# Moving one product of the second matmul stage into the first, with a new order of the rest, in a fused attention and MLP kernel

## The chip, the core and the metric

The kernel runs on one core of a Trainium2 chip. The core has five engines, each with its own queue of instructions in program order: TensorE (PE, with weight loads as PEld), VectorE (DVE), ScalarE (ACT), GpSimd (POOL) and SyncE (SP), which here issues the transfers. They meet only at semaphores. Matmuls write to PSUM, eight banks of 128 x 512 float32, from which VectorE and ScalarE read. The metric is the device time of one execution in microseconds (us).

## What is computed

Attention inside chunks of 64 tokens, then an MLP with exact Gelu over all tokens:

```python
q_c = q.reshape(B, H, nc, chunk, D)          # B, H, S, D = 8, 8, 576, 64; chunk = 64
scores = scale * np.matmul(q_c, k_c.transpose(0, 1, 2, 4, 3))
attn = np.exp(scores - np.max(scores, axis=-1, keepdims=True))
attn = attn / (np.sum(attn, axis=-1, keepdims=True) + 1e-09)
out = np.matmul(attn, v_c)
...
h = x @ w_in                                 # x: 4608 x 512, w_in: 512 x 2048
g = 0.5 * h * (1.0 + erf(h * inv_sqrt2))
return (g @ w_out).astype(np.float32)        # w_out: 2048 x 512
```

x is the attention output with its eight heads side by side.

## The kernel before

**Tiles.** The 4608 tokens are nine tiles of 512 (t = 0 to 8, so the fourth to eighth are t = 3 to 7). Tile t < 8 holds eight of the nine chunks of batch t; the ninth tile gathers the last chunk of all batches. While the MLP of tile t runs, the attention of tile t + 1 is fitted in between, so that its x is ready for the next tile, and with `quad_S` the scores of tile t + 2.

**Two stages.** `mm1_groups` computes h with Gelu, then `mm2_seven` (from t = 3) the output rows. Both use a block scheme in which a 2 by 2 block product takes seven products instead of eight, with sums of blocks formed beforehand (of x: `x_sums`; of w_in and w_out: once; of h: `h_sums` in three parts h1 to h3, `h_third`, `h_fourth`) and sums of results afterwards. In mm1 the columns of h fall into four groups a to d, each with seven products of four matmuls (128 x 256). In mm2 each of the seven products is 16 matmuls of that size.

**mm1's order** is written out as a string of words (`FOUR` for t = 3 to 8, line 639), which line 686 walks. `3b` is product 3 of group b on TensorE; products 1, 2 go to the group's bank X, 3, 5, 6 to Y, 4, 7 to Z. `c1b` is ScalarE's copy of X to Y, `c2b` and `c3b` are copies of Y to SBUF (ScalarE, VectorE), `a1b` and `a2b` are VectorE's adds of Z to those, `g12b` is a Gelu on ScalarE that writes a quarter of the group's h (g11 from X, g12 from Y, g21 and g22 from the sums that a2 and a1 leave). `h1` to `h3` (lines 576, 577) are VectorE's sums of h that mm2's second and third factors need. The order of the words is the order of each engine's queue.

**mm2's order** (line 761 on). The banks X, Y, Z, W are taken in turn from the pool `ps_mm`, which has three banks and which mm1 uses for its four Y banks (a, b, c, d) before. So X reuses the bank of group b's Y, read last by g12b, Y that of c, Z that of d, and W that of X. Before the change, with the lines:

- X1 (781): the first product, into X; then ScalarE copies X to Y (782), so that both can go on from the same term.
- hook 1: `act_table(Exp)`, then `rows_av` (line 334: 64 small matmuls on TensorE, attention times v of the next tile, into two `ps_tp` banks, three `ps_at` banks and mm2's Z bank) and `rows_x` (line 352: for each of these six banks a reciprocal and a multiply on VectorE; after the third and the sixth bank a transpose by DMA on SP writes half of x).
- `h_third` on VectorE; Y2 (787) into Y, and ScalarE copies it to s2 (788).
- X2 (789) into X, ScalarE copies it to y (790), SP stores it.
- Y1 (792) into Y, ScalarE copies it to s5 (793); `h_fourth`.
- hook 2: loads of later tiles on SP. Z (796) into Z; between its two halves, from t = 4 on, hook (2, 0): `quad_S`, 64 small matmuls for the scores of tile t + 2 into two `ps_tp` and two `ps_at` banks, their exponentials on ScalarE, `act_table(Gelu)`. At t = 3 it stands ahead of Z. VectorE adds Z to s2 (797).
- W (800) into a new bank; VectorE adds it to s5 and s2 (801, 802), SP stores. hook 4: `x_sums` of the next tile.
- Y4 (805) into Y; ScalarE copies it to y, SP stores.

The last tile goes through `last_seven` instead. The eighth (t = 7) has no `quad_S`, as no tile t + 2 is left.

**Pools that set waits.** `ps_mm` three banks, `ps_at` three, `ps_tp` two. The tiles `y_sb` (two), `x_t` (one, shared by the rows that `rows_x` writes and the sums of x), h (one), and one buffer for each sum of h.

Of the kernel before, what the change touches and what calls it, by code (L numbers as in the profile page):

```python
# [11 lines left out]
def kernel(  # L12
# [10 lines left out]
    P = 128  # L23
    f32 = mybir.dt.float32
# [327 lines left out]
    def rows_x(t):  # L352

        st = tiles[t]
        rows = work.tile([P, 2, 2 * G, 2, D], bf16, tag="x_t", name="x_r", bufs=1)
        xT = by_halves(t).rearrange("p s g (n e) -> p s (g n) e", e=P)
        for bank in range(6):
            s, b0 = bank // 3, NX * (bank % 3)
            nb = min(NX, 2 * G - b0)
            av = st["av"][bank][:, :2 * nb]  # L360
            one = work.tile([P, 2 * NX], f32, tag="one", name="one", bufs=2)
            nc.vector.reciprocal(one[:, :2 * nb], av[:, :, D])
            nc.vector.tensor_tensor(rows[:, s, b0:b0 + nb].rearrange("p b r d -> p (b r) d"), av[:, :, :D],
                                    one[:, :2 * nb].to_broadcast([P, 2 * nb, D]), op=mybir.AluOpType.mult)
            if bank % 3 == 2:
                nc.sync.dma_start_transpose(xT[:, s], rows[:, s].rearrange("p b r d -> p (b r d)"))
# [248 lines left out]
    def x_sums(t, which=(1, 3, 2, 4)):  # L615
# [7 lines left out]
        for i in which:  # L623
# [17 lines left out]
               g22c 4d g12c g12b 3d a2c a2d g21c g22d g12d g21d h2 h3"""  # L641

    FOURS = range(FIRST7, NT)
    PROGRAMS = {1: LATE, 2: THIRD, **{t: FOUR for t in FOURS}}

    def mm1_groups(t, extra, between={}):
# [39 lines left out]
        for word in PROGRAMS.get(t, PROGRAM).split():  # L686
# [71 lines left out]
    def halves(bank):  # L758
        return [bank[:, 0], bank[:, 1]]

    def mm2_seven(t, at={}):

        def also(i):
            for u in at.get(i, ()):
                u()
        st = tiles[t]
        h = st["h"][:].rearrange("p (k f) (m e) -> p k f m e", k=2, m=2)
        w = w_out_sb[:].rearrange("p (k f) (n e) -> p k f n e", k=2, n=2)
        T = [None] + [w_t[i] for i in range(1, 5)]
        def bank_mm():  # L770
            return ps_mm.tile([P, 2, NH], f32, tag="mm", name="y_ps")
# [10 lines left out]
        AC(Y[:], X[:])  # L782
# [12 lines left out]
        also(2)  # L795
        product(halves(Z), h[:, 1, :, 1], T[4], True, lambda m: also((2, m)))
        TT(s2[:], Z[:], s2[:], op=add)
        also(3)
# [166 lines left out]
    with tc.manual_schedule():  # L965
# [126 lines left out]
        for t in range(1, NT):  # L1092
# [30 lines left out]
            elif n < NT:  # L1123
# [91 lines left out]
```

## Time and profile before

| | us |
|---|---|
| median of three executions | 271.12 |
| lowest, highest | 270.23, 272.2 |
| the profiled execution | 270.41 |
| its span, first to last instruction | 268.6 |
| TensorE busy | 259.6 (97%) |
| VectorE busy | 202.1 (75%) |
| ScalarE busy | 187.1 (70%) |
| GpSimd busy | 77.0 (29%) |

The profile is one execution. A row of its timeline has the start from the span's beginning, the duration, the engine, the kernel's line, the operation, output and input by the program's names with the shape, and how many instructions were merged; in brackets how long the engine stood before it and what ended that. A bar of matmuls shows also the pipeline's tail, so successive bars overlap; the step from one start to the next is the slot that TensorE spends. The chain of waits follows the work that ended last back from the end, at each step to what released it. The granted clock of TensorE is given in tenths for 40 slices of the span.

In the middle of the span the tiles repeat each 26.3 us (Y2 starts at 149.67 in one and at 175.94 in the next).

### The profile page before, as it was taken

How to read it: one execution, taken by the hardware profiler on the slowest of the kernel's cores; microseconds unless marked ns; L12 is line 12 of the kernel's file. 1: busy time of each engine (PE TensorE's matmuls, PEld its weight loads, DVE VectorE, ACT ScalarE, POOL GpSimd, SP SyncE). 2: the span in 40 equal slices, each digit the busy share in tenths (PEclk: the TensorE clock that was granted, in tenths of full speed). 3: DMA queues.
4: the chain of work that ended last, by engine and by line, in shares of the span. 5: the costliest groups of instructions: out<-in, count | busy, mean ns of one | idle time of the engine just before them, and what ended most of it. 6: DMA issues, size and time to landing. Idle time of an engine off the chain costs nothing.

```text
span 268.6 us, 7554 instructions
## 1 busy us (share of the span) xinstructions
PE 259.6 (97%) x3077; PEld 195.6 (73%) x3092; DVE 202.1 (75%) x372; ACT 187.1 (70%) x364; POOL 77.0 (29%) x130
## 2 busy tenths in 40 slices
PE   7989999999999999999999999999999999999993
PEld 3554454476548654888888888888888888888882
DVE  2565775989997879589569956995699769958961
ACT  3466756797767967897689669957995799239700
POOL 3735667361440061441044103500362030000000
PEclk9999999999999999999999999999999999999998
DMA  7999999997979959999899989988886760430005
GB/s 230 285 377 402 395 388 243 237 286 194 336 205 261 244 123 231 279 237 191 232 232 231 177 216 242 264 152 206 237 193 146 166 192 0 89 138 12 2 2 156
DMA packets 127075, 56.59 MB, mean 211 GB/s; under 512 B 103488, under 2 KB 120896, under 8 KB 127040
## 3 DMA queue, kind: packets, MB, share of 16 engines
q1 hardware_dynamic: 126592, 55.59, 79.4%
q10 hardware_dynamic: 448, 0.52, 0.7%
q8 instruction: 24, 0.39, 0.6%
q14 instruction: 11, 0.09, 0.1%
HBM read 36.70 MB, written 9.44 MB: 172 GB/s over the span
## 4 chain that ended last, share of the span: by engine, by line
PE 92%; ACT 2%; DVE 1%; DMA 1%; issue 1%; POOL 0%; SPq 0%; ACTq 0%; DVEq 0%; POOLq 0%
PE y_ps L746 24%; PE h_Y L677 15%; PE y_ps L866 12%; PE h_Z L677 10%; PE h_X L677 10%; PE h_ps L538 6%; PE y_ps L891 4%; PE y_ps L755 4%; PE s_ps L247 2%; PE h_ps L699 1%; DMA arrival<-in_k_dram 1%; PE tp L170 1%; ACT y_ps L782 1%; PE warm L958 1%; PE rc_ps L484 1%
## 5 line engine op out<-in xcount | busy, mean ns | idle before, releaser
L677 PEld LDWEIGHTS <-w_in_s 128*128 128x128 bf16 x480 | 46.8, 98 | 6.1
L677 PEld LDWEIGHTS <-w_in_sb 128*128 128x128 bf16 x360 | 35.1, 98 | 6.5
L677 PE MATMUL h_X<-x,w_in_sb 128*128 128x256 bf16 x240 | 33.7, 272 | 0.0
L677 PE MATMUL h_Y<-x_t,w_in_s 128*128 128x256 bf16 x240 | 32.7, 272 | 0.0
L866 PE MATMUL y_ps<-w_out_sb,h 128*128 128x512 bf16 x137 | 31.7, 379 | 0.9 <-issue 0.8
L746 PEld LDWEIGHTS <-h_s 128*128 128x128 bf16 x304 | 29.7, 98 | 3.6 <-issue 0.2
L746 PEld LDWEIGHTS <-h 128*128 128x128 bf16 x288 | 27.8, 98 | 3.4
L218 POOL CAST v_nat<-arrival 128x1024 bf16<-128x1024 f32 x14 | 14.8, 1061 | 48.4 <-DMA arrival<-in_v_dram 48.3
L164 POOL CAST q_nat<-arrival 128x512 bf16<-128x512 f32 x33 | 19.4, 627 | 28.2 <-DMA arrival<-in_q_dram 19.1
L164 POOL CAST k_nat<-arrival 128x512 bf16<-128x512 f32 x34 | 21.9, 678 | 14.0 <-DMA arrival<-in_k_dram 10.1
L746 PE MATMUL y_ps<-w_t,h_s 128*128 128x256 bf16 x208 | 24.8, 273 | 0.0
L866 PEld LDWEIGHTS <-h 128*128 128x128 bf16 x144 | 13.3, 98 | 15.0 <-issue 0.2
L746 PE MATMUL y_ps<-w_out_sb,h 128*128 128x256 bf16 x192 | 22.9, 273 | 0.0
L963 ACT ACT_TABLE_LOAD x16 | 20.5, 1283 | 1.0 <-PEq L1199 0.7
L684 ACT ACTIVATE h<-h_Y 128x512 bf16<-128x512 f32 x30 | 17.7, 595 | 2.4 <-PE h_Y L677 1.9
L714 ACT COPY h_Y<-h_X 128x512 f32<-128x512 f32 x30 | 17.0, 582 | 2.8 <-PE h_X L677 2.6
L684 ACT ACTIVATE h<-h_X 128x512 bf16<-128x512 f32 x30 | 17.8, 597 | 1.4 <-PE h_X L677 0.6
L677 PE MATMUL h_Z<-x_t,w_in_s 128*128 128x256 bf16 x120 | 18.0, 273 | 0.0
L677 PE MATMUL h_Y<-x,w_in_s 128*128 128x256 bf16 x120 | 17.7, 273 | 0.0
L677 PE MATMUL h_Z<-x_t,w_in_sb 128*128 128x256 bf16 x120 | 17.4, 272 | 0.0
L725 DVE COPY h_a<-h_Y 128x512 f32<-128x512 f32 x8 | 5.5, 692 | 14.1 <-PE h_Y L677 14.1
L254 ACT ACTIVATE pT<-s_ps 128x512 bf16<-128x512 f32 x28 | 14.5, 601 | 2.3 <-PE s_ps L247 2.3
(148 smaller groups left out, 489.4 us busy)
## 6 DMA issues: line engine op xcount, KB each, us to landing
arrival<-in_q_dram SPq DMA_DIRECT2D x7, 1024.0 KB
arrival<-in_k_dram SPq DMA_DIRECT2D x24, 256.0 KB
out_dram<-y_sb SPq DMA_DIRECT2D x23, 256.0 KB
arrival<-in_v_dram SPq DMA_DIRECT2D x20, 256.0 KB
arrival<-in_moe_w_out_dram SPq DMA_DIRECT2D x4, 1024.0 KB
arrival<-in_v_dram SPq DMA_DIRECT2D x30, 128.0 KB
out_dram<-y_sb SPq DMA_DIRECT2D x5, 512.0 KB
arrival<-in_moe_w_in_dram SPq DMA_DIRECT2D x4, 512.0 KB
```

Source lines behind the costliest of these rows:

```text
L164: copy(st[nm][:, g].rearrange("p j r d -> p r j d"), st[nm + "f"][:, 2 * g:2 * g + 2])
L218: copy(st["v"][:, part[0], part[1], :D], st["vf"][:, part[0], part[1]])
L254: nc.scalar.activation(pT[:].rearrange("p u (c j) -> p u c j", j=J), s_ps[g2][c][:].rearrange("p u (j c) -> p u c j", j=J), Act.Exp, scale ...
L538: nc.tensor.matmul(h_ps[a][:], w_in_sb[:, ks, f * P:(f + 1) * P], st["x"][:, ks, :], start=(ks == 0), stop=(ks == KS - 1))
L677: nc.tensor.matmul(banks[g + name][:, i], lhs[:, kk, i], rhs[:, kk], start=fresh and i == kk == 0, stop=(kk == 1), skip_group_check=True)
L684: nc.scalar.activation(h[:, j:j + 2, m], src[:], Act.Gelu)
L714: AC(banks[g + "Y"][:], banks[g + "X"][:])
L746: nc.tensor.matmul(out[m], lhs[:, f, m * P:(m + 1) * P], rhs[:, f, :], start=fresh and f == 0 and (m == 0 or len(out) == 3), stop=(f == FH ...
L755: nc.tensor.matmul(out[m], lhs[:, f, m * P:(m + 1) * P], rhs[:, f, :], start=False, stop=(f == FH - 1), skip_group_check=True)
L866: nc.tensor.matmul(y_ps[:], st["h"][:, f, ms * P:(ms + 1) * P], w_out_sb[:, f, :], start=(f == 0), stop=(f == FF - 1))
L891: nc.tensor.matmul(tiles[t]["y_ps", ms][:], tiles[t]["h"][:, f, ms * P:(ms + 1) * P], w_out_sb[:, f, :], start=(f == 0), stop=False)
L963: nc.scalar.activation(act_scratch[:], rest[:, 0:1], func)
```

## The change

For the tiles t = 3 to 7 a new program string `AHEAD` takes the place of `FOUR`. It is the same up to `c3d`. Behind that, products 3b, 3c, 4c come in this order, then the word `X`, which is mm2's first product (X1), then 4d and 3d. The word `cX` is ScalarE's copy of X to Y. The word h2 stands ahead of a2d, h3 at the end. `mm2_seven` then starts with X2, and its order becomes X2, AV, Y2, Z, Y1 (with `quad_S` between its halves, at t = 3 too), W, Y4. `h_third` follows Z's matmuls in program order, and `h_fourth` Z's add. The s5 copy of bank Y is on VectorE instead of ScalarE. In `rows_x` the bank order is 5, 3, 4, 0, 1, 2 (bank 5 is mm2's Z), in the tiles t + 1 = 4 to 8. The ninth tile keeps `FOUR` and `last_seven`.

```diff
-        for bank in range(6):
+        for at, bank in enumerate((5, 3, 4, 0, 1, 2)):
...
-            if bank % 3 == 2:
+            if at % 3 == 2:
                 nc.sync.dma_start_transpose(xT[:, s], rows[:, s].rearrange("p b r d -> p (b r d)"))
...
+    AHEAD = """begin 1a 1b c1a 1c 6a 7a c1b c2a 6b 5a 2a c1c 6c c2b 5b 7b c3a g11a a1a c3b c2c 3a a1b 1d 4a g22a 4b
+               g12a c1d 2b a2a g22b 6d 5c g21a a2b 2d 7c h1 g11b c3c c2d 2c g11d 5d a1c 7d c3d 3b g21b g11c 3c a1d
+               g22c 4c g12b X g12c a2c 4d g22d g21c cX h2 a2d 3d g12d g21d h3"""
...
-    PROGRAMS = {1: LATE, 2: THIRD, **{t: FOUR for t in FOURS}}
+    PROGRAMS = {1: LATE, 2: THIRD, **{t: AHEAD if t < B else FOUR for t in FOURS}}
...
+            elif word == "X":
+                mm2_first(t)
+            elif word == "cX":
+                st["Y"] = bank_mm()
+                AC(st["Y"][:], st["X"][:])
...
+    def mm2_first(t):
+        h, w = out_blocks(t)
+        tiles[t]["X"] = bank_mm()
+        product(halves(tiles[t]["X"]), h[:, 0, :, 0], w[:, 0, :, 0], True)
...
-        X, Y = bank_mm(), bank_mm()
+        X, Y = (st["X"], st["Y"]) if t < B else (bank_mm(), bank_mm())
...
-        also(0)
-        product(halves(X), h[:, 0, :, 0], w[:, 0, :, 0], True)
-        AC(Y[:], X[:])
         Z = bank_mm()
         st["Z"] = Z[:].rearrange("p m n -> p (m n)")
+        product_by_f(halves(X), h[:, 1, :, 0], w[:, 1, :, 0])
+        AC(y[0][:, :, :NH], X[:])
+        store(t, 0, 0, y)
         also(1)
-        h_third(t)
         product_by_f(halves(Y), h_sum(t, 2), T[2])
         AC(s2[:], Y[:])
-        product(halves(X), h[:, 1, :, 0], w[:, 1, :, 0], False)
-        AC(y[0][:, :, :NH], X[:])
-        store(t, 0, 0, y)
-        product(halves(Y), h_sum(t, 1), T[1], False)
-        AC(s5[:], Y[:])
+        product(halves(Z), h[:, 1, :, 1], T[4], True)
+        h_third(t)
+        TT(s2[:], Z[:], s2[:], op=add)
         h_fourth(t)
         also(2)
-        product(halves(Z), h[:, 1, :, 1], T[4], True, lambda m: also((2, m)))
-        TT(s2[:], Z[:], s2[:], op=add)
+        product(halves(Y), h_sum(t, 1), T[1], False, lambda m: also((2, m)))
+        DV(s5[:], Y[:])
         also(3)
...
-                    e2.setdefault(2 if t == FIRST7 else (2, 0), []).extend([lambda: quad_S(n + 1), lambda: act_table(Act.Gelu)])
+                    e2.setdefault((2, 0), []).extend([lambda: quad_S(n + 1), lambda: act_table(Act.Gelu)])
```

`TT` is VectorE's two-input operation, `DV` and `AC` are copies on VectorE and ScalarE, `product_by_f` walks the 16 matmuls by blocks of h's columns, both row halves in turn, and `product` one row half after the other.

More of the change, by code (lines that the diff above doesn't have):

```diff
@@ L759, in halves, with bank_mm, out_blocks @@
         return [bank[:, 0], bank[:, 1]]
+    def bank_mm():
+        return ps_mm.tile([P, 2, NH], f32, tag="mm", name="y_ps")
+    def out_blocks(t):
+        return (tiles[t]["h"][:].rearrange("p (k f) (m e) -> p k f m e", k=2, m=2),
+                w_out_sb[:].rearrange("p (k f) (n e) -> p k f n e", k=2, n=2))
+    def mm2_first(t):
+        h, w = out_blocks(t)
+        tiles[t]["X"] = bank_mm()
+        product(halves(tiles[t]["X"]), h[:, 0, :, 0], w[:, 0, :, 0], True)
     def mm2_seven(t, at={}):
@@ L766, in mm2_seven @@
         st = tiles[t]
-        h = st["h"][:].rearrange("p (k f) (m e) -> p k f m e", k=2, m=2)
-        w = w_out_sb[:].rearrange("p (k f) (n e) -> p k f n e", k=2, n=2)
+        h, w = out_blocks(t)
         T = [None] + [w_t[i] for i in range(1, 5)]
-        def bank_mm():
-            return ps_mm.tile([P, 2, NH], f32, tag="mm", name="y_ps")
-        X, Y = bank_mm(), bank_mm()
+        X, Y = (st["X"], st["Y"]) if t < B else (bank_mm(), bank_mm())
         s2, s5 = (work.tile([P, 2, NH], f32, tag=nm, name=nm, bufs=1) for nm in ("y_2", "y_5"))
```

## The prediction

> **What bounds the kernel now.** I read the page first, its busy shares, its clock row and the chain that ended last:
>
> ```profile
> PE 259.6 (97%) x3077; PEld 195.6 (73%) x3092; DVE 202.1 (75%) x372; ACT 187.1 (70%) x364; POOL 77.0 (29%) x130
> ...
> PEclk9999999999999999999999999999999999999998
> ...
> PE 92%; ACT 2%; DVE 1%; DMA 1%; issue 1%; POOL 0%; SPq 0%; ACTq 0%; DVEq 0%; POOLq 0%
> ```
>
> TensorE (PE) is busy 97% of the span, its clock is never held down, and 92% of the chain is its own work. The change removes no matmul, so all that can move is the little time in which PE stands. To see how little, I take the chain of waits and the PE timeline of the sixth tile (t = 5, whose second stage begins at 173.31). I name mm2's seven products by bank and term: X1 (line 781), Y2 (787), X2 (789), Y1 (792), Z (796), W (800), Y4 (805); AV and S are the next tiles' attention products (L347, L247). The chain around AV:
>
> ```profile
> 175.32 0.58 ACT y_ps L782
> 175.90 0.04 issue
> 175.94 1.91 PE y_ps L755 x16
> ```
>
> And PE alone:
>
> ```profile
> 149.67 1.91 PE L755 MATMUL y_ps<-w_t,h_s 128*128 128x256 bf16 x16
> 151.42 1.91 PE L746 MATMUL y_ps<-w_out_sb,h 128*128 128x256 bf16 x16
> ...
> 154.91 1.04 PE L746 MATMUL y_ps<-w_t,h 128*128 128x256 bf16 x8
> 155.88 0.74 PE L247 MATMUL s_ps<-q_t,k_t 64*64 64x64 bf16 x64
> 156.55 1.05 PE L746 MATMUL y_ps<-w_t,h 128*128 128x256 bf16 x8
> ...
> 171.07 0.60 PE L677 MATMUL h_Y<-x,w_in_s 128*128 128x256 bf16 x4
> ...
> 171.94 0.60 PE L677 MATMUL h_Y<-x,w_in_s 128*128 128x256 bf16 x4
> 172.44 0.60 PE L677 MATMUL h_Z<-x_t,w_in_sb 128*128 128x256 bf16 x4
> 172.88 0.60 PE L677 MATMUL h_Y<-x,w_in_s 128*128 128x256 bf16 x4
> 173.31 1.91 PE L746 MATMUL y_ps<-w_out_sb,h 128*128 128x256 bf16 x16
> 175.16 0.60 PE L347 MATMUL av_ps<-v_nat,pT 64*64 64x65 bf16 x50
> ```
>
> A product of 16 matmuls takes its slot of 1.75 (149.67 to 151.42), 0.109 a matmul, and four take 0.44 (172.44 to 172.88). S, 64 small matmuls, costs 0.77: half of Z would end its slot at 154.91 + 0.87 = 155.78, and Z's other half starts at 156.55. AV, also 64 small ones, costs 173.31 to 175.94 less 1.75, which is 0.88. So beyond what S costs, AV has 0.11 of waiting for ScalarE's copy X to Y (L782, to 175.90). The step from 171.94 to 172.44 is 0.50, so product 4d waits 0.06. That is the idle time a changed tile can give back here: 0.17, and five tiles change.
>
> **The new order up to AV.** I walk the sixth tile with old durations. The old slots of 3c, 4c, 3b become 3b 171.07, 3c 171.51, 4c 171.94; then X1 172.38, 4d 174.13, 3d 174.57, X2 175.00. Each has to meet ScalarE and VectorE:
>
> ```profile
> 171.02 0.63 ACT L684 ACTIVATE h<-h_sb 128x512 bf16<-128x512 f32 x1
> 171.71 0.60 ACT L684 ACTIVATE h<-h_Y 128x512 bf16<-128x512 f32 x1
> ...
> 174.12 0.59 ACT L684 ACTIVATE h<-h_Y 128x512 bf16<-128x512 f32 x1
> 174.59 0.63 ACT L684 ACTIVATE h<-h_d 128x512 bf16<-128x512 f32 x1
> ```
>
> ```profile
> 171.70 0.69 DVE L728 TENSOR_TENSOR h_d<-h_Z,h_d 128x512 f32<-128x512 f32 x1
> ...
> 173.08 0.69 DVE L728 TENSOR_TENSOR h_d<-h_Z,h_d 128x512 f32<-128x512 f32 x1
> 173.69 0.68 DVE L576 TENSOR_TENSOR h_s<-h 128x1024 bf16<-128x1024 bf16 x1
> 174.40 0.69 DVE L577 TENSOR_TENSOR h_s<-h_s,h 128x1024 bf16<-128x1024 bf16 x1
> 175.01 0.42 DVE L576 TENSOR_TENSOR h_s<-h 128x512 bf16<-128x512 bf16 x1
> ```
>
> X1 takes the bank that g12b reads. A Gelu starts 0.04 behind its product's end (171.07 + 0.60 = 171.67, 171.71), so g12b, whose product now has that slot, ends at 172.31: X1 does not wait, with 0.07 to spare. X1 ends at 172.38 + 1.91 = 174.29. The copy starts 0.10 behind (before: 175.22, 175.32), takes 0.58 and frees PE 0.04 later: 175.01. Thus its cover is no longer AV but 4d and 3d, 0.88 of slots, and it fits to 0.01. 4d no longer waits, for a1d is done at 172.39: -0.06.
>
> X2 reads the last Gelu, g21d, in its 13th to 16th matmul, from 175.01 + 12 x 0.109 = 176.32. Ahead of g21d stands a2d, and ahead of a2d on VectorE now h2. a2c starts at 171.94 + 0.60 + 0.10 = 172.64, h2 0.61 later (as 173.08 to 173.69) at 173.25, and takes 1.32 (173.69 to 175.01) to 174.57; a2d waits for 4d anyway, to 174.83, and ends at 175.52. g12d starts at 174.57 + 0.60 + 0.04 = 175.21, g21d 0.47 later (174.12 to 174.59) and ends at 176.31. PE waits 0.03. X2's slot ends at 176.79, AV costs 0.77, Y2 starts at 177.56. Before, the same work (Y2's slot for X2's) was done at 175.94 + 1.75 = 177.69. So **-0.13 a tile**, and five tiles give **-0.65**.
>
> **From AV to the next tile.** Count from Y2's start. Behind AV there are now five products where there were six, and VectorE still owes the same list, plus the s5 copy that ScalarE had (no price there, ScalarE has room):
>
> ```profile
> 149.54 0.19 DVE L362 RECIPROCAL one<-av_ps 128x6 f32<-128x6 f32 x1
> ...
> 153.41 1.21 DVE L581 TENSOR_TENSOR h_s<-h 128x2048 bf16<-128x2048 bf16 x1
> 154.55 1.22 DVE L585 TENSOR_TENSOR h_s<-h,h_s 128x2048 bf16<-128x2048 bf16 x1
> 157.70 0.69 DVE L797 TENSOR_TENSOR y<-y_ps,y 128x512 f32<-128x512 f32 x1 [1.94 <-PE y_ps L746]
> 159.44 0.69 DVE L801 TENSOR_TENSOR y_sb<-y_ps,y 128x512 f32<-128x512 f32 x1 [1.04 <-PE y_ps L746]
> 160.04 0.68 DVE L802 TENSOR_TENSOR y_sb<-y_ps,y 128x512 f32<-128x512 f32 x1
> 160.64 0.75 DVE L625 TENSOR_TENSOR x_t<-x 128x512 bf16<-128x512 bf16 x2
> ...
> L725 DVE COPY h_a<-h_Y 128x512 f32<-128x512 f32 x8 | 5.5, 692 | 14.1 <-PE h_Y L677 14.1
> ```
>
> Bank 5 is filled last, so the reading now starts only when AV is done: 0.07 + 0.10 = 0.17. The six banks take 153.41 - 149.54 = 3.87, to 4.04; h_third 1.14 to 5.18; Z's add 0.60 to 5.78; h_fourth 1.14 to 6.92; the s5 copy 0.69 (the L725 row) to 7.61; PE may go at 7.65. PE itself: Y2, Z, Y1 and S, 3 x 1.75 + 0.77 = 6.01, W to 7.75, then Y4, which overwrites the bank just copied. In the fourth to seventh tile Y4 finds the copy done with **0.10 to spare: 0**. Z's bank (5) is read by 0.8, and Z starts at 1.75. S reuses banks 0 and 2; bank 2 is read last, to about 4.1, and S starts at 4.46: 0.
>
> The eighth tile has no S, for no tile is left to prepare. There PE runs products back to back:
>
> ```profile
> 233.78 1.91 PE L746 MATMUL y_ps<-w_t,h 128*128 128x256 bf16 x16
> 235.53 1.91 PE L746 MATMUL y_ps<-w_t,h_s 128*128 128x256 bf16 x16
> ```
>
> W would end its slot at 4 x 1.75 = 6.99 and VectorE is not through before 7.65: **+0.66**, a wait that the old order, with six products behind AV, did not have.
>
> The x transposes are queued on SP behind the store of X2's half, whose copy is done at 0.08; rows for the first are ready at 2.1, for the second at 4.1. Y2 starts 177.56 - 175.94 = 1.62 later than before and the rows, which began 0.13 ahead of it (149.54, 149.67), 0.17 behind it: SP's loads behind the transposes go out up to 1.9 later. Landings aren't in the rows, only bounds are:
>
> ```profile
> 203.27 1.32 SPq L197 DMA_TRANSPOSE k_t<-k_nat  x1
> ...
> 208.48 0.74 PE L247 MATMUL s_ps<-q_t,k_t 64*64 64x64 bf16 x64
> ```
>
> k_t was read 5.21 after its transpose was issued, so 5.2 is the most. W's add starts at 7.75 + 0.16 + 0.10 = 8.01, x's sums 1.20 behind it (159.44 to 160.64) at 9.21, 5.1 after the issue; the next tile's products start at 9.50, and 6a, the first that needs the sums, is three products later. So 0 even at the bound. The k_t of these rows is read by S of the seventh tile, which now comes 0.2 earlier, while k may arrive up to 1.9 later: between 0 and 2.1, once. I take 0, nearest to x's transposes, which nobody waited for in five tiles.
>
> One more unknown is GpSimd. In the seventh tile its casts of k ran beside h2:
>
> ```profile
> 199.85 3.39 POOL L164 CAST k_nat<-arrival 128x512 bf16<-128x512 f32 x4 [1.56 <-DMA arrival<-in_k_dram]
> ...
> 199.95 1.05 DVE L576 TENSOR_TENSOR h_s<-h 128x1024 bf16<-128x1024 bf16 x1
> ```
>
> 1.05 instead of 0.68. Before, nothing on PE hung on h2 there; now g21d does. Both adds of h2 stretched by 0.37 end at 175.31, put a2d 0.48 later and PE's wait at about 0.35; casts that start 1 us later miss half of h2. I take +0.1 between 0 and 0.35.
>
> The sum: -0.65 + 0.66 + 0.1 = **+0.1 us**. On the profiled execution, 270.41 (span 268.6), that is 270.5. The four executions shown (270.23, 270.41, 271.12, 272.2) have their middle at 270.8, so I forecast 270.9.
>
> **The rivals.** *First, slower: VectorE becomes the bound from AV to Y4.* Its spare is 0.10 in four tiles and less than nothing in the eighth; past that, each delay goes to the end one for one. If one of the two large adds (1.21 and 1.22) met a GpSimd cast in each tile and stretched as L576 did, by 1.05/0.68, it would cost 0.66: 4 x 0.56 + 0.66 = 2.9, so 273.8; half as much gives about 272.2. For it: the chain is without any gap. Against: no cast row lies between 4 and 7 us behind AV in these tiles. Chance 0.14. *Second, faster: the waits that fit to hundredths do not show and the eighth tile's is smaller*, as when the bank readings overlap more. Without that wait, five times the whole 0.17 is -0.85: 269.9. Chance 0.18. *Third: h2 is held off by the casts, each add for a whole cast*, 3.39/4 = 0.85. Then a2d starts at 173.25 + 1.32 + 1.70 = 176.27 instead of 174.83, and the seventh tile loses 1.4: 272.2. Against it: the row shows 0.37 more, not 0.85. Chance 0.06. On this last the Trainium skill, "SBUF — State Buffer", section "Who interferes with whom", says that a VectorE instruction with two SBUF inputs and a GpSimd instruction that reads SBUF exclude each other, the later one blocked until the first is through; the trace agrees that they meet (1.05 against 0.68). By that rule alone the sum would be the third rival's 272.2.
>
> **How the numbers follow.** The forecast has 0.62, with its own range 270.0 to 271.8: 0.9 either side for the spread of the four executions and for ends that fit to hundredths in five tiles. Down to 269.6 the second rival is mostly held, up to 272.3 the third and the lower half of the first; the upper half, and k_t late by its full 2.1, are what it leaves out, under 0.2 in all. 1%, 2.7 us, is about what a measurement of this kernel can tell from no change. Slower by more takes the first rival at full size, half of its 0.14: 0.07. Faster by more would take 0.54 a tile where 0.17 is idle around these words: 0.02. Within: 0.91.
>
> **What would show it.** Right: Y2 comes 0.77 behind X2's slot in each changed tile, L782's copy gone from the chain; VectorE has no gap from AV to the s5 copy; in the eighth tile PE waits about 0.6 for that copy ahead of Y4, in the others not. Wrong: a PE wait ahead of X1 or X2, a wait of Y4 in the fourth to seventh tile, S waiting for bank 2, or x's sums waiting for a transpose; any of them over 0.5 a tile breaks the forecast.

## The result, and the profile after

The changed kernel takes 272.64 us (median; 271.05 to 274.38) where the kernel before, on the same chip, takes 270.77 (269.39 to 273.48). The ratio is 1.0064, with a 95% interval of 1.0040 to 1.0088: about 1.7 us slower. That is inside the 1% that the prediction called "within", but 0.8 us over the upper end of the forecast's own range (271.8), and 0.3 over the 272.3 up to which it held its rivals.

The profiled execution took 271.72, with a span of 269.93 against 268.58 before, so it shows 1.35 of the 1.7. Its page:

```profile
PE 258.9 (96%) x3077; PEld 194.2 (72%) x3092; DVE 206.5 (76%) x377; ACT 185.0 (69%) x359; POOL 77.0 (29%) x130
...
PEclk9999999999999999999999999999999999999997
```

TensorE still runs at full clock and is busy 96%. VectorE has five instructions more (377 for 372) and ScalarE five fewer (359 for 364): the s5 copy, once in each of five tiles. These two counts, which look like bookkeeping, will matter.

To find the time, I lay the tiles side by side by the start of mm1's first products (the x12 rows of `h_X<-x,w_in_sb` in TensorE's timeline), each tile up to the next, the ninth up to the end of VectorE's last add, and from there to the end of the span:

| us | 4th starts | 4th | 5th | 6th | 7th | 8th | 9th | end |
|---|---|---|---|---|---|---|---|---|
| before | 108.40 | 26.26 | 26.27 | 26.26 | 26.34 | 25.49 | 25.38 | 4.18 |
| after | 108.52 | 26.18 | 26.20 | 26.20 | 26.20 | 26.10 | 25.73 | 4.79 |

Four tiles gained 0.06 to 0.14 each (0.35 in all), the eighth lost 0.61, the ninth, whose code isn't changed, 0.35, and the end, which isn't changed either, 0.61. With 0.12 from before the fourth tile these make the 1.35.

**The changed tiles went nearly as walked.** TensorE in the sixth tile after the change:

```profile
172.35 1.91 PE L755 MATMUL y_ps<-w_out_sb,h 128*128 128x256 bf16 x16
174.10 0.60 PE L681 MATMUL h_Z<-x_t,w_in_sb 128*128 128x256 bf16 x4
174.54 0.60 PE L681 MATMUL h_Y<-x,w_in_s 128*128 128x256 bf16 x4
174.98 1.98 PE L764 MATMUL y_ps<-w_out_sb,h 128*128 128x256 bf16 x16
176.89 0.60 PE L347 MATMUL av_ps<-v_nat,pT 64*64 64x65 bf16 x50
177.58 1.92 PE L764 MATMUL y_ps<-w_t,h_s 128*128 128x256 bf16 x16
```

These are X1, 4d, 3d, X2, AV and Y2; the prediction had X1 at 172.38, X2 at 175.00 and Y2 at 177.56. 4d follows X1 by a full slot and no more (174.10 - 172.35 = 1.75), so its wait of 0.06 is gone. AV's first row now stands 177.58 - 176.89 = 0.69 ahead of Y2, where it stood 175.94 - 175.16 = 0.78 ahead before, so the wait for the copy of X to Y is gone too. But from X2's start to that row it takes 176.89 - 174.98 = 1.91, where X1 before took 175.16 - 173.31 = 1.85. The weight loads of X2 show the 0.06:

```profile
174.87 1.30 PEld L764 LDWEIGHTS <-h 128*128 128x128 bf16 x12
176.34 0.33 PEld L764 LDWEIGHTS <-h 128*128 128x128 bf16 x4 [0.17 <-ACT h L688]
```

X2's last four matmuls wait for the last Gelu, g21d. The 13th matmul starts at 176.34, where the 12th (176.18) and the pace of 0.109 would have had it at 176.28. The prediction allowed 0.03 for this. X2's slot is 1.81 with it, and from its end AV costs 0.79 in the fourth to seventh tile (0.76 in the eighth), close to the 0.77 of the walk. So the step that fell short is X2's wait for g21d, in each of the five tiles.

**The eighth tile** shows the new wait in the chain of waits (start, duration, what):

```profile
237.00 0.61 DVE y L812
237.62 0.04 issue
237.66 1.91 PE y_ps L755 x16
```

L812 is the s5 copy, now on VectorE, and the matmuls behind it are Y4. W's slot ended at 237.00, so TensorE stands 0.66, just what the prediction has for it.

**The ninth tile** is unchanged code, and its loss stands in one place, the same chain further on:

```profile
250.16 0.37 issue
250.53 0.70 DVE h_d L737
251.23 0.04 issue
251.27 0.60 PE h_Z L681 x4
```

"issue" is time in which the engine waited for nothing that the profile shows. The timeline of VectorE has the same add (a1d) after and before the change:

```profile
249.38 0.69 DVE L734 COPY h_d<-h_Y 128x512 f32<-128x512 f32 x1 [0.16 <-PE h_Y L681]
250.53 0.69 DVE L737 TENSOR_TENSOR h_d<-h_Z,h_d 128x512 f32<-128x512 f32 x1 [0.46 <-PE h_Y L681]
```

```profile
249.00 0.69 DVE L725 COPY h_d<-h_Y 128x512 f32<-128x512 f32 x1 [0.16 <-PE h_Y L677]
249.79 0.69 DVE L728 TENSOR_TENSOR h_d<-h_Z,h_d 128x512 f32<-128x512 f32 x1
```

Before, it follows its copy by 0.79; after, by 1.15. TensorE's 4d waits for it.

**The end** differs in ScalarE's queue of stores. After the change and before:

```profile
261.94 4.33 ACTq L862 DMA_DIRECT2D out_dram<-y_sb  x4
```

```profile
261.20 3.96 ACTq L847 DMA_DIRECT2D out_dram<-y_sb  x4
```

The same four stores take ScalarE 0.37 longer to issue, and the span ends 0.61 later behind VectorE's last add. There is one more sign. In the DMA view one transfer of 8 KB of instruction code (queue q14) falls between 264 and 268 after the change, among the last stores:

```profile
q14 instruction: 1, 0.01, 0.5%
```

In the kernel before, the same view has it between 253 and 259, with no transfer of the kernel beside it.

### The profile page after: what moved, and what is told of

It is laid out like the page before. It is cut to its first block, busy times and chain, and to the rows that moved or that the text cites. A ratio compares the mean times of both kernels' runs of the same rounds, so it can differ in the third digit from the quotient of the medians.

```text
span 269.9 us, 7554 instructions
## 1 busy us (share of the span) xinstructions
PE 258.9 (96%) x3077; PEld 194.2 (72%) x3092; DVE 206.5 (76%) x377; ACT 185.0 (69%) x359; POOL 77.0 (29%) x130
## 5 line engine op out<-in xcount | busy, mean ns | idle before, releaser
L881 PEld LDWEIGHTS <-h 128*128 128x128 bf16 x144 | 13.3, 98 | 15.0 <-issue 0.2
L755 PEld LDWEIGHTS <-h 128*128 128x128 bf16 x208 | 20.3, 98 | 2.4
L681 PE MATMUL h_Y<-x,w_in_s 128*128 128x256 bf16 x120 | 16.9, 273 | 0.0
L538 PE MATMUL h_ps<-x,w_in_sb 128*128 128x512 bf16 x67 | 15.0, 379 | 0.1
```

Of the source, the lines that this page charges most:

```text
L538: nc.tensor.matmul(h_ps[a][:], w_in_sb[:, ks, f * P:(f + 1) * P], st["x"][:, ks, :], start=(ks == 0), stop=(ks == KS - 1))
L681: nc.tensor.matmul(banks[g + name][:, i], lhs[:, kk, i], rhs[:, kk], start=fresh and i == kk == 0, stop=(kk == 1), skip_group_check=True)
L755: nc.tensor.matmul(out[m], lhs[:, f, m * P:(m + 1) * P], rhs[:, f, :], start=fresh and f == 0 and (m == 0 or len(out) == 3), stop=(f == FH ...
L881: nc.tensor.matmul(y_ps[:], st["h"][:, f, ms * P:(ms + 1) * P], w_out_sb[:, f, :], start=(f == 0), stop=(f == FF - 1))
```

## The experiments

All ratios are to the kernel before, taken on the same chip between the others; the interval is 95%. Each run's profile gives a row of this table (us, as above):

| | 4th starts | 4th | 5th | 6th | 7th | 8th | 9th | end | time | ratio |
|---|---|---|---|---|---|---|---|---|---|---|
| r_same | 108.55 | 26.89 | 26.52 | 26.20 | 26.69 | 26.07 | 25.73 | 4.77 | 271.96 | 1.0050 (1.0026 to 1.0075) |
| e8_act | 109.10 | 26.35 | 26.20 | 26.20 | 26.57 | 25.50 | 25.38 | 4.78 | 271.91 | 1.0041 (1.0010 to 1.0072) |
| e_pad | 108.14 | 26.19 | 26.20 | 26.20 | 26.65 | 26.36 | 25.72 | 4.19 | 271.62 | 1.0028 (1.0000 to 1.0055) |
| b_dv | 108.64 | 26.28 | 26.26 | 26.27 | 26.26 | 25.49 | 25.73 | 4.18 | 270.92 | 1.0013 (0.9988 to 1.0038) |
| e_best | 108.41 | 26.64 | 26.20 | 26.19 | 26.21 | 25.49 | 25.38 | 4.20 | 270.67 | 1.0025 (1.0002 to 1.0048) |
| e_best_r | 108.32 | 26.19 | 26.22 | 26.20 | 26.20 | 25.49 | 25.38 | 4.20 | 270.63 | 1.0003 (0.9970 to 1.0035) |
| e_store | 107.81 | 27.05 | 26.38 | 26.19 | 26.29 | 25.78 | 25.38 | 4.19 | 271.08 | 1.0038 (1.0013 to 1.0063) |
| e_early | 109.45 | 26.38 | 26.35 | 26.20 | 26.26 | 25.48 | 25.38 | 4.19 | 270.27 | 1.0010 (0.9983 to 1.0037) |
| e_v1 | 109.13 | 26.71 | 26.20 | 26.20 | 26.69 | 25.49 | 25.39 | 4.20 | 274.11 | 1.0104 (1.0058 to 1.0151) |
| e_v8 | 108.07 | 26.19 | 26.30 | 26.20 | 26.21 | 25.50 | 25.39 | 4.20 | 270.89 | 1.0004 (0.9969 to 1.0040) |
| e_v8_r | 108.60 | 26.19 | 26.33 | 26.20 | 26.46 | 25.50 | 25.37 | 4.20 | 270.74 | 0.9998 (0.9969 to 1.0027) |
| e_vall | 108.59 | 26.18 | 26.47 | 26.20 | 26.73 | 25.50 | 25.37 | 4.21 | 270.84 | 0.9989 (0.9959 to 1.0019) |
| e_banks | 108.82 | 28.18 | 28.33 | 28.18 | 28.26 | 27.41 | 25.72 | 4.80 | 281.52, once | |
| e_dve1 | 107.59 | 26.48 | 26.45 | 26.21 | 26.44 | 25.50 | 25.38 | 4.19 | 270.02, once | |
| e_dve2 | 114.84 | 27.25 | 26.69 | 26.20 | 27.35 | 25.78 | 25.73 | 4.32 | 279.95, once | |

The intervals are some 0.3% (0.8 us) to either side, as wide as the single effects. So the sizes below come from the tiles of the profiles, and the ratios only have to agree with them.

### The changed kernel again (r_same)

> The changed kernel once more. Theory A (what the one profile shows is what the change does): against before, the start of the ninth tile comes about 0.4 later, of which the eighth tile's wait of Y4 for VectorE is 0.6 and the four other tiles give back 0.06 to 0.14 each; the ninth tile's VectorE add of group d starts 0.4 late; and from the last VectorE add's end to the span's end it takes 4.8 instead of 4.2, with an instruction transfer (q14) between 264 and 268. Theory B (chance): the late add in the ninth tile and the longer end are single events of that execution, and are not seen here; then the measured 1.7 must come from elsewhere, for instance from transfers of x that land late in other executions.

The eighth and ninth tile and the end repeat to 0.03. But the fourth, fifth and seventh tile are now 0.3 to 0.7 slower than in the first profile. TensorE at the end of the fourth:

```profile
135.44 1.48 PE L681 MATMUL h_X<-x,w_in_sb 128*128 128x256 bf16 x12 [0.54 <-DMA x<-x_r]
```

It waits for x, a transpose by DMA. (The bracket counts from the end of the bar before, so the slot lost is 0.16 more, 0.70.) SP's queue ahead of that, then the same rows in a run in which nothing waits (e_best_r, below):

```profile
124.37 1.59 SPq L197 DMA_TRANSPOSE k_t<-k_nat  x1
126.01 2.21 SPq L144 DMA_DIRECT2D arrival<-in_v_dram  x2
128.32 0.83 SPq L872 DMA_DIRECT2D out_dram<-y_sb  x1
129.24 2.97 SPq L366 DMA_TRANSPOSE x<-x_r  x2
```

```profile
119.46 1.97 SPq L197 DMA_TRANSPOSE k_t<-k_nat  x1
121.48 1.20 SPq L144 DMA_DIRECT2D arrival<-in_v_dram  x2
125.01 0.38 SPq L872 DMA_DIRECT2D out_dram<-y_sb  x1
127.26 3.17 SPq L366 DMA_TRANSPOSE x<-x_r  x2
```

In r_same the k transpose goes out at 124.37, 4.9 later, and all behind it is pushed: x's transposes at 129.24, 2.0 later. By the trace's marks the second of them also takes longer to land, 4.8 us against 3.3. The seventh tile ends with such a wait too (0.32 in the bracket). So this wait comes and goes from one execution to the next, with when k arrives.

The fifth tile has another wait, of X1 for the Gelu g12b, whose bank it takes (a slot of 0.33):

```profile
143.91 0.71 DVE L577 TENSOR_TENSOR h_s<-h_s,h 128x512 bf16<-128x512 bf16 x1
147.22 1.91 PE L755 MATMUL y_ps<-w_out_sb,h 128*128 128x256 bf16 x16 [0.16 <-ACT h L688]
```

Here the two adds of h1 ran beside GpSimd's casts of k and took 0.89 and 0.71, each 0.42 where nothing runs beside it. Over the fifth tiles of seven runs X1's wait is what h1 is stretched by, less 0.43: stretches of 0.53 to 0.76 give 0.10 to 0.33, and at 0.45 or less X1 doesn't wait. The prediction considered the casts beside h2 and, in a rival, beside the two large adds behind AV; beside h1 it had none, and X1 had 0.07 to spare.

### The s5 copy of the eighth tile back on ScalarE (e8_act)

```diff
-        DV(s5[:], Y[:])
+        (AC if t == B - 1 else DV)(s5[:], Y[:])
```

> In the eighth tile alone the s5 copy of bank Y is back on ScalarE, which has no exponentials there. Theory A: Y4 no longer waits for VectorE's queue, the ninth tile starts 0.6 earlier than in the changed kernel (about 0.2 earlier than before), and the time falls by 0.6, to 1.004 of before. Rival: Y4's factor, h_fourth, is then late by as much (it is next in VectorE's queue), and under 0.2 is won.

The eighth tile takes 25.50, as before the change, so Y4's wait was its whole loss. The ninth falls back to 25.38 with it, and the end stays at 4.78. The ratio is 1.0041 beside r_same's 1.0050, a difference that lies inside the intervals. In its profile the fourth tile is 0.15 over the 26.20 of a tile without waits (Y4 there waits for VectorE; see e_store), and the seventh 0.37. TensorE, GpSimd and SP in the seventh:

```profile
209.34 0.74 PE L247 MATMUL s_ps<-q_t,k_t 64*64 64x64 bf16 x64 [0.27 <-DMA k_t<-k_nat]
```

```profile
202.75 2.77 POOL L164 CAST k_nat<-arrival 128x512 bf16<-128x512 f32 x4 [3.80 <-DMA arrival<-in_k_dram]
```

```profile
205.55 1.39 SPq L197 DMA_TRANSPOSE k_t<-k_nat  x1
```

S waits for k_t: the k of the ninth tile arrives late, its cast starts at 202.75 (199.85 before the change) and its transpose at 205.55 (203.27), in a tile that itself starts 0.7 later.

### ScalarE's count restored (e_pad)

The changed kernel with five copies of one column on ScalarE at the start, so that ScalarE issues as many instructions as before the change:

```diff
+        for _ in range(5):
+            AC(act_scratch[:], rest[:, 0:1])
```

> The changed kernel with five one-element copies more on ScalarE at the very start, where ScalarE waits for the first loads, so that ScalarE has as many instructions as before. Theory C (instruction count): the change takes five instructions from ScalarE, so ScalarE reaches the border of its next block of code five instructions later, among the last stores, and the block's transfer (q14) delays one transfer engine there. Then here q14 moves back to about 254, the end takes 4.2 instead of 4.8, and 0.6 is won against the changed kernel. Rival (chance or order of the stores): the end stays at 4.8, or was 4.8 only once.

The end returns to 4.19, and the last four stores are issued as before the change:

```profile
262.27 3.96 ACTq L862 DMA_DIRECT2D out_dram<-y_sb  x4
```

The transfer of code (q14) is back between 253 and 256. So 0.6 us of the loss come from how many instructions ScalarE had issued ahead of the stores, and hang on nothing that the change orders. The ninth tile stays at 25.72. The eighth is 0.26 slower still: X1 waits there, behind an add of h1 that took 1.07 instead of 0.42 beside a cast of v. The seventh has S waiting for k_t again (0.38).

### The kernel before, with the s5 copy on VectorE alone (b_dv)

```diff
-        AC(s5[:], Y[:])
+        DV(s5[:], Y[:])
```

> The kernel before with only the s5 copy of bank Y moved from ScalarE to VectorE in the fourth to eighth tile; the order of the products is the old one. Theory C: ScalarE has five instructions fewer, the q14 transfer falls among the last stores, the end takes 4.8, and the time is 0.6 over before, though no wait is new. Rival: the copy is free, the end stays at 4.2 and the time is that of before, 1.000.

No changed tile gains or loses (26.26 to 26.28, eighth 25.49): in the old order VectorE has room for the copy. It has room for more: in the fourth tile `h_fourth` (129.78) took 2.09 instead of 1.21 beside a cast of v, and k's transpose came 3.0 later than in the first profile of this order (122.60 against 119.59), and nothing on TensorE waited. The ninth tile takes 25.73, with the same late a1d:

```profile
250.32 0.69 DVE L728 TENSOR_TENSOR h_d<-h_Z,h_d 128x512 f32<-128x512 f32 x1 [0.45 <-PE h_Y L677]
```

So the ninth tile's 0.35 needs no new order either; five more instructions on VectorE are enough. The end stays at 4.18. ScalarE lost five copies here but gained five semaphore rows, and has 458 rows in the trace as before the change, where the changed kernel has 453. So what counts is every row of an engine, the semaphores too, which the page of the profile leaves out; by instructions alone the end would have been expected at 4.8.

### Both repaired (e_best)

e8_act with four such copies at the start:

> Three repairs at once: the eighth tile's s5 copy on ScalarE (VectorE then has four instructions more than before instead of five), and four one-element copies at the start on ScalarE, so that its count is that of before. Theory: the three fixed losses go, 0.6 in the eighth tile, 0.35 at VectorE's late add in the ninth, 0.6 at the end; what is left is landing, transposes of x and k that come late by up to 0.7 in the fourth, fifth or seventh tile, and the gain of 0.06 to 0.14 a tile. So the end takes 4.2, the ninth tile's length to the last add is 25.4, and the ratio to before is 0.998 to 1.002. Rival (the losses are not additive, PE just waits elsewhere): the ratio stays at 1.003 or more without any landing wait in the trace.

The eighth tile 25.49, the ninth 25.38, the end 4.20, and three tiles at 26.19 to 26.21. What is left is one wait for x, 0.30 at 135.05, at the end of the fourth. The time is 270.67, 1.0025.

### SP's store behind x's transposes (e_store)

As it ran, this is e8_act with five copies at the start, so it also has the eighth tile's s5 copy on ScalarE, and in all changed tiles

```diff
-        store(t, 0, 0, y)
         also(1)
+        store(t, 0, 0, y)
```

> The changed kernel with ScalarE's count restored (five copies at the start), and in the five tiles SP's store of X2's half put behind the two transposes of x, as it was before. Landing theory: in the seventh tile, where k's transpose, this store and x's transposes follow each other on SP, x's transposes are issued 0.6 earlier (205.9 instead of 206.6), and a wait of the next tile's first product, where there is one, shrinks by as much; k_t's landing, and the wait of S for it, stay. Time against e_pad: 0 to -0.4. Rival: the transposes are held by the transfer engines, not by SP's order, and land as late as before.

1.0038, no better than e_best. x's transposes of the seventh tile go out 0.4 earlier (206.75 against 207.16), but the second of them lands no sooner (213.3 against 213.1 by the trace's marks). The fourth tile is slow, 27.05. Its timeline has another reason (GpSimd, VectorE, TensorE):

```profile
130.34 1.05 POOL L218 CAST v_nat<-arrival 128x1024 bf16<-128x1024 f32 x1 [6.96 <-DMA arrival<-in_v_dram]
130.53 1.93 DVE L585 TENSOR_TENSOR h_s<-h,h_s 128x2048 bf16<-128x2048 bf16 x1
132.38 0.68 DVE L812 COPY y<-y_ps 128x512 f32<-128x512 f32 x1
133.11 1.91 PE L755 MATMUL y_ps<-w_out_sb,h_s 128*128 128x256 bf16 x16 [0.47 <-DVE y L812]
```

v arrived so late that its cast met `h_fourth` (L585), which took 1.93 instead of 1.21; the s5 copy and Y4 waited behind it. That is the first rival's mechanism. It stands in the fourth tile of e8_act, e_early and e_dve1 too: `h_fourth` took 0.26, 0.25 and 0.37 longer beside the cast of v, and Y4's slot came 0.17, 0.17 and 0.29 late (here 0.72 and 0.63). So the spare that the prediction put at 0.10 measures 0.08 to 0.09, and past it the delay goes on one for one. The Trainium skill, "SBUF — State Buffer", section "Who interferes with whom", has it that an add with two SBUF inputs, started behind a GpSimd read, is blocked until that read is through. The trace agrees about in size: the cast had 130.34 + 1.05 - 130.53 = 0.86 to go, and the add took 0.72 longer. In the other three the cast had 0.39, 0.38 and 0.52 to go, so each add was held for the rest of the cast less about 0.14.

### The seventh and eighth tile in the old order (e_early)

The change for t = 3 to 5 only, with `FOUR`, the old mm2 order and the old bank order for t = 6 and 7, and three copies at the start.

```diff
-    FOURS = range(FIRST7, NT)
-    PROGRAMS = {1: LATE, 2: THIRD, **{t: AHEAD if t < B else FOUR for t in FOURS}}
+    FOURS, NEW = range(FIRST7, NT), 6
+    PROGRAMS = {1: LATE, 2: THIRD, **{t: AHEAD if t < NEW else FOUR for t in FOURS}}
...
```

> The new order only in the fourth to sixth tile; the seventh and eighth run the order of before, banks and copies included; three copies at the start restore ScalarE's count. Theory: the eighth tile's wait is gone, S of the seventh waits for no k_t and its successor for no x; the sixth to ninth tile steps are 26.3, 26.3 and 25.5 as before, the fourth and fifth 26.2 unless x lands late. VectorE's count is three over before. Ratio 0.998 to 1.002. If it is 1.003 or more, something else than the named waits costs.

1.0010. The eighth tile, the ninth and the end are as before the change, and the seventh's wait for k_t is gone. In the fourth and fifth tile 0.15 to 0.18 remain over the 26.20 of a tile without waits: Y4 waits 0.17 for VectorE in the fourth, X1 0.15 in the fifth.

### AV's banks read in the old order (e_banks)

```diff
-        for at, bank in enumerate((5, 3, 4, 0, 1, 2)):
+        for at, bank in enumerate(range(6)):
```

> The changed kernel with attention's banks read in the old order, 0 to 5, so that mm2's Z bank is read last. Theory: Z waits for bank 5, read about 4.0 behind Y2's start instead of 0.8, so PE stands 2.3 in each of five tiles, and the rest of VectorE's list moves no further; span 11 longer than the changed kernel's, some of it won back where PE waited for VectorE anyway: 278 to 282. Rival: other waits take it up, under 275.

281.52. In each changed tile Z waits for bank 5, which is now read last:

```profile
185.75 1.91 PE L755 MATMUL y_ps<-w_t,h 128*128 128x256 bf16 x16 [1.85 <-DVE x_r L363]
```

The loss is 2.0 to 2.1 in each of four tiles and 1.3 in the eighth. So it is the new order of the reads that lets Z stand second behind AV. (This is a single execution.)

### VectorE's rows, one more and two more (e_dve1, e_dve2)

e_best has 471 rows of VectorE in its trace, the changed kernel 472. e_dve1 adds a small copy at the start, which brings a semaphore row along (473); e_dve2 adds a memset that waits for nothing (472):

```diff
+        DV(act_scratch[:], rest[:, 0:1])                  # e_dve1
+        nc.vector.memset(dve_scratch[:], 0.0)             # e_dve2
```

> As the kernel with the s5 copy of the eighth tile on ScalarE and four small ScalarE copies at the start (e_best), plus one small VectorE copy at the start, so that VectorE again issues five more instructions than before the change instead of four. Nothing else is touched. If a fixed place in VectorE's stream costs it 0.36 to 0.40 us, as in the traces in which VectorE has five more, the first add behind TensorE's wait in the ninth tile (a1d) starts that much later than its inputs allow again and the ninth tile takes 25.73 us instead of 25.38; the tail behind VectorE's last add stays at 4.2. If instead the late add comes from where the s5 copy stands, the ninth tile stays at 25.38.

> As e_best (s5's copy of the eighth tile on ScalarE, four small ScalarE copies at the start), plus one small VectorE memset at the start which waits for nothing, so that VectorE's stream has one row more than e_best's in the trace: 472, as in the changed kernel. The small copy of e_dve1 had brought a semaphore row along, 473. If VectorE loses 0.36 to 0.40 us at a fixed row of its stream (the 448th), the add a1d of the ninth tile, which stands there with 472 rows and directly behind a wait, starts that much late and the ninth tile takes 25.73 us, between two kernels (471 and 473 rows) that take 25.38. If the late add came with the s5 copy on VectorE in the eighth tile instead, which no kernel of these three has, it takes 25.38 here as well. The tail stays 4.2 in both.

e_dve1 has the ninth tile at 25.38. That tells nothing against the count, since its row count came out at six over the kernel before (467) instead of the five that the expectation states. e_dve2 has 472, and takes 25.73. VectorE in e_dve1, then in e_dve2:

```profile
248.65 0.69 DVE L734 COPY h_d<-h_Y 128x512 f32<-128x512 f32 x1 [0.16 <-PE h_Y L681]
249.44 0.69 DVE L737 TENSOR_TENSOR h_d<-h_Z,h_d 128x512 f32<-128x512 f32 x1
```

```profile
258.09 0.69 DVE L734 COPY h_d<-h_Y 128x512 f32<-128x512 f32 x1 [0.16 <-PE h_Y L681]
259.23 0.69 DVE L737 TENSOR_TENSOR h_d<-h_Z,h_d 128x512 f32<-128x512 f32 x1 [0.46 <-PE h_Y L681]
```

In six traces a1d is the 448th row of VectorE (the changed kernel, r_same, e_pad, b_dv, e_banks, e_dve2), and it starts 1.15 behind its copy. In the other eleven it is the 443rd, 446th, 447th or 449th, and starts 0.80 behind. Three of these (e_v8, e_v8_r, e_vall) have 472 rows as well, but the row more stands behind a1d; so what counts is the rows ahead of it. Neither the order nor the s5 copy's place is needed for it. The 279.95 of e_dve2 is a single execution: its fourth tile starts at 114.84, some six us later than elsewhere, and its fourth to seventh tile lose 2.7 to waits of the kinds above. Whether the memset has a part in that isn't known; the run was made for the ninth tile alone.

### The loads beside x's transposes (e_v1, e_v8, e_best_r, e_v8_r, e_vall)

e_v1 is e_best with the second half of v loaded ahead of AV instead of behind x's transposes:

```diff
-                e2 = {1: [lambda: rows_av(n, tiles[n - 1]["Z"]), lambda: rows_x(n)], 2: [], 3: [], 4: [lambda: x_sums(n)]}
-                e2[2] += [next_q, next_k, rest_of_v] if t + 3 < B else [rest_of_v, next_q]
+                e2 = {1: [rest_of_v, lambda: rows_av(n, tiles[n - 1]["Z"]), lambda: rows_x(n)], 2: [], 3: [], 4: [lambda: x_sums(n)]}
+                e2[2] += [next_q, next_k] if t + 3 < B else [next_q]
```

> As e_best, with the loads of the second half of v (three or four transfers on SyncE, 1.9 us of its time in the sixth tile) moved from behind x's transposes to ahead of the attention's product with v, where SyncE stands idle from 178.6 to 180.2 in e_best. If SyncE's place in its queue is what brings k late, the loads of k and its cast come up to 1.9 earlier, the transpose to k_t of the seventh tile is issued near 203 instead of 204.88 and S does not wait; where the traces of the changed kernel show TensorE waiting for k_t or x by 0.1 to 0.7 us in one or two tiles, at most x's wait is left: 270.2 to 270.6 beside a kernel before of 270.4. If the loads ahead hold up x's transposes instead, the products of mm1 at the start of the next tile wait, by 0.3 to 1 us a tile in up to four tiles: 271 to 274.

274.11, a ratio of 1.0104 (1.0058 to 1.0151): the slowest of the versions that ran more than once. k did come earlier (its transpose in the seventh tile at 203.11 instead of 204.88, and S doesn't wait), but x's transposes went out later (209.56 there, 207.16 in e_best), and mm1 waits for them in two tiles, here at the end of the fourth:

```profile
135.84 1.48 PE L681 MATMUL h_X<-x,w_in_sb 128*128 128x256 bf16 x12 [0.37 <-DMA x<-x_r]
```

The profiled execution, 271.8, was the fastest of six, so how far such waits go in the others isn't seen.

e_v8 moves the v loads of the seventh tile the other way, behind the sums of x; e_vall does the same in the fourth and fifth tile too (there the condition is `t + 3 != B and t < B - 1`). e_best_r and e_v8_r repeat e_best and e_v8 beside it:

```diff
+                if t + 2 == B:
+                    e2[2].remove(rest_of_v)
+                    e2[4] += [rest_of_v]
```

> As e_best, with the four loads of the ninth tile's v that follow x's transposes in the seventh tile moved behind the sums of x, so that nothing is loaded while x's second transpose is on its way. If these loads share the transfer engines with it, x's second transpose in the seventh tile lands about 3.1 us after its issue, as in the eighth tile where no load follows, instead of 4.3 (e_best), and the eighth tile's first products never wait for it; over the whole kernel this is worth 0 to 0.4 us. If the transposes are slow for another reason, the landing stays at 4.3 and the time at that of e_best, 1.0025 of the kernel before.

> e_best again (s5's copy of the eighth tile on ScalarE, four small ScalarE copies at the start), beside e_v8 and e_vall on one chip, since its 1.0025 and e_v8's 1.0004 come from different calls. If the loads behind x's transposes are what is left of the loss, it comes out above e_v8_r again, by 0.1 to 0.3 per cent. If nothing but chance lies between them, the two ratios agree within 0.1 per cent.

> e_v8 again (e_best with the ninth tile's four v loads moved from behind x's transposes of the seventh tile to behind the sums of x). With the loads as the cause: ratio 0.999 to 1.001, below e_best_r by 0.1 to 0.3 per cent. Without: as e_best_r.

> e_v8 with the same move in the fourth and fifth tile too (three v loads each, from behind the k loads to behind the sums of x). There the loads of q and k still follow x's transposes directly, and v's come 6 us later, when x has landed. If only loads that are under way together with a transpose slow it, the move in these tiles changes nothing: as e_v8_r. If each load less on SyncE between a transpose and the next helps, it is 0.1 per cent faster than e_v8_r. Should v come too late for its casts in the next tile, the attention's product with v waits there and the kernel is slower than e_best_r.

Measured side by side, e_best_r has 1.0003, e_v8_r 0.9998 and e_vall 0.9989, all within one another's intervals. So it isn't shown to matter whether these loads stand behind x's transposes or behind the sums of x, and e_best's 1.0025 against its repeat's 1.0003 can be chance between two measurements. Nor did x's second transpose land in the 3.1 us expected with loads as the cause: by the trace's marks it took 3.9 in e_v8 and 4.5 in e_v8_r. In e_v8_r and e_vall, S waits for k_t in the seventh tile (0.19 and 0.46), in e_best_r and e_v8 not.

The profile of e_best_r is the change without any of its mishaps: tiles of 26.19 to 26.22, eighth and ninth as before the change, a span of 268.19 against 268.58. That is all there was to gain, 0.3 us in the tiles and 0.1 ahead of them, 0.14% together, and in the times it doesn't come out: no version here is faster than the kernel before by more than its interval.

## Why the prediction was wrong

Forecast 270.9 (+0.1), measured +1.7. By its own steps:

- **"So -0.13 a tile, and five tiles give -0.65".** The starts came out to 0.03 and the sign was right; the size was 0.06 to 0.08 in the fourth to sixth tile, 0.35 in the four tiles with S. The seventh gained 0.14, as in the old order it had lost 0.06 to Y2 waiting for the sums of h beside the casts. The two waits to be saved were read rightly: 4d's 0.06 and AV's 0.11 are gone. What failed is "PE waits 0.03": X2 waits 0.06 for g21d and its slot is 1.81 instead of 1.78. With AV at 0.79 instead of 0.77, and some 0.01 behind Y2, the 0.13 becomes 0.06.
- **"W would end its slot at 6.99 and VectorE is not through before 7.65: +0.66".** Right: Y2 at 229.99, Y4 at 237.66, 7.67 later, TensorE stands 0.66; e8_act takes it away (26.10 to 25.50).
- **"0.10 to spare: 0" for Y4 in the fourth to seventh tile.** Right in the first profile, and the spare measures 0.08 to 0.09. It was too thin for a cast of v that comes late: Y4 waits 0.17 to 0.63 in the fourth tile of e8_act, e_early, e_dve1 and e_store.
- **"X1 does not wait, with 0.07 to spare".** Right in the first profile; X1 waits 0.10 to 0.33 in the fifth tile of seven runs, r_same first, and 0.29 in the eighth of e_pad and e_store, behind adds of h1 stretched by casts. No term of the sum had that.
- **h2 beside the casts, "+0.1 between 0 and 0.35".** 0 beyond X2's 0.06 in the first profile; ahead of X2's last matmuls a wait of 0.29 in the fourth tile of e_store and of 0.30 in the seventh of e_v1. (Of the old order the prediction said that "nothing on PE hung on h2 there"; not quite, as Y2's 0.06 stood behind these sums.)
- **x's transposes, "So 0 even at the bound", and k_t, "between 0 and 2.1, once. I take 0".** These steps failed. Waits for x of 0.3 to 0.5 stand in r_same, e_best and e_v1, and waits of S for k_t of 0.2 to 0.5 in e8_act, e_pad, e_v8_r, e_vall and e_dve1. The walk counted x's transposes from when their rows are ready; where k is late, SP is still busy with what it issues ahead of them. And one execution's rows can't bound a landing. The old order had slack for late k: in b_dv, with k 3.0 later, x's second transpose of the fourth tile went out at 128.79 and nothing waited; in r_same it went out at 130.63. The two profiles of the old order have no wait of this or the kinds just named, but two are few. How much of the 1.7 all such waits make on average is only an estimate, 0.5: what is left of 1.7 when the settled terms (0.61 + 0.35 + 0.61 - 0.35 = 1.22) are taken off, and by the interval of the ratio it could be anything from 0 to 1.2. The profiles agree: in the changed kernel, r_same, e8_act, e_pad, e_best and e_best_r these waits sum to between 0 and 1.5 us, 0.5 on average, half of it for x, the rest for k_t, X1 and Y4.
- **What no step had: the number of instructions on each engine.** "The s5 copy that ScalarE had (no price there, ScalarE has room)" was taken as work alone. But with 472 rows on VectorE its 448th falls on a1d of the ninth tile, 0.35 (e_dve2 and b_dv against their neighbours), and with 453 on ScalarE the last stores and a transfer of code meet at the end, 0.61 (e_pad and b_dv). Together, 0.96, they are over half of the miss of 1.6.

The rivals: VectorE as the bound from AV to Y4 was seen in one tile each of several runs, by the mechanism named, but not in the first profile and never in each tile; of the 0.85 that the second rival would gain, 0.35 came; h2 held off by whole casts was not seen, as an add waits out only the rest of the cast that it meets. The cause that decided was none of them.

## What to carry to other kernels

In a kernel whose chain has no gaps, a move that saves 0.1 us a tile must be priced with what it takes from the slack of the transfers, and a landing time seen in one execution is no bound for it: look at what its queue holds ahead of it and how that shifts when an earlier load is late. Before a small loss in code that wasn't touched is put down to the new order, compare the number of rows of each engine, semaphores included, and restore it by an instruction or two at the start: here two such shifts cost 1 us. And where a walk fits to hundredths, each margin has to be held against what can stretch the work ahead of it: here the casts that ran beside VectorE's sums ate the 0.07 of X1 and the 0.10 of Y4.

## What the runs showed of the hardware

**A fixed row of an engine's stream is late.** VectorE's 448th row begins some 0.35 late where it is an add directly behind a wait: in six traces out of six, and not where that add is the 447th or the 449th. In ScalarE's stream of the changed kernel the third of the last four stores is the 448th row, and those four take 4.33 instead of 3.96 to issue. With five rows more (e_pad) the 448th falls into ScalarE's idle time ahead of the stores, and nothing is lost; in e_best it is the first of the four, and they take 3.95. Where the row follows others closely, as on VectorE in the kernel before, it isn't late at all. The Trainium skill, "Runtime: NRT & Kernel Launch", section "Instruction fetch mechanics", says that an engine's instructions are fetched in blocks of 256 while it executes, and that crossing from one block to the next is mostly hidden. The trace agrees that code is fetched during the run (the q14 row above), though each transfer of that queue is of 8 KB where the section has blocks of 16 KiB, and "mostly" is where it adds a number: 0.35 on VectorE and up to 0.6 at the end, when the place isn't hidden. That the 448th recorded row is such a border is argued, not shown, as not every instruction has a record.

**An add beside a cast is held for the rest of the cast.** The four rows of `h_fourth` under e_store, and that of b_dv (1.02 of the cast to go, 0.88 longer), all show the rest of GpSimd's cast less about 0.14. Whether it costs anything is the order's affair: in b_dv 0.88 cost nothing, in e_store 0.72 cost 0.63.

**The end of the kernel is sensitive to the place of a row, too.** Of the 0.61, 0.37 is the late issue on ScalarE; the other 0.24 comes behind it, while the code transfer shares the engines with the last stores. Those two were never had apart.
